# RWKV-7 with a hardswish feed-forward on one core: PSUM read in pairs of banks, and three steps moved in the head

## The chip, the core and the metric

One core of a Trainium2 chip runs the whole program. The metric is the device time in microseconds. Three runs of the kernel before took 807.92, 809.98 and 811.37 us; the median is 809.98. The engines are named as in the profile: PE multiplies matrices (PEld is its weight load), DVE, ACT and POOL work element by element, SP issues transfers, as ACT's queue also can.

## What is computed

```python
for t in range(S):                                   # S=768, per batch (4) and head (8), D=40
    y[:, :, t] = np.einsum('bhd,bhde->bhe', rt, state)
    Sa = np.einsum('bhde,bhe->bhd', state, at)
    state = state * wt[:, :, None, :] - np.einsum('bhd,bhe->bhde', Sa, bt) \
            + np.einsum('bhd,bhe->bhde', vt, kt)
x = y.transpose(0, 2, 1, 3).reshape(3072, 320)
h = x @ w_in                                          # 320 -> 2048
out = (h * np.clip(h + 3.0, 0.0, 6.0) / 6.0) @ w_out  # 2048 -> 320
```

The recurrence is in float32; the feed-forward weights arrive in 8-byte form and are turned to float32 on the chip.

## The kernel before, in words

Time is cut into blocks of 64 steps. A **unit** holds one such block of two batches and all 8 heads, 128 rows in all; there are 24 units, four to a group (NU = 4). Units 0 to 3 are the first group.

For each unit, `prepare` makes what doesn't depend on the state. Stage W transposes w on PE, ACT (for unit 0 DVE) copies it into `wm`, and a scan on DVE (L507) makes running products. Stage gam makes the reverse scan (L518) and fills the halves of `gam` and `rgam`, two by DVE (L526, L527) and two by POOL (L528, L529). A and B transpose a and b and multiply by `gam` and `rgam` on DVE (L544, L552), after a memset of some columns of `wm` (L541). F multiplies the two into a triangular matrix that ACT copies out of PSUM. K, factor, E and EV treat k and v: DVE copies E under a mask (`masked`, L483), POOL makes `KBt` (L621).

`invert` inverts the triangles of a group of four units. It begins with a DVE transpose `fb` (L679), makes some sixty dependent pairs of DVE instructions (L699, L705) and ends with two transposes `tb` and `tt` (L708, L713). Other DVE work is put between its instructions by `aside`. `third_blocks` (X for units 0 and 1, Y for 2 and 3) completes the inverse `tinv` with PE (L734, L757) and ACT (L742, L767). Before that, POOL sets all of `tinv` to zero (L1196), after the first two weight pieces, whose raw form lay there, have been converted.

`step` runs the part that depends on the state: RT and VT (transposes of r and v), C (a masked product of the two), R, U, UT, S, rS, sn (new state, L917), H (masked) and y; then `move` sends y as `xt` to the feed-forward by eight transfers on SP.

`feed_forward` yields pieces: `expand` (L1017, four pieces and a narrow rest, into two banks h), ACT and DVE make the activation (L1032, L1033), `contract` (L1058) sums into bank o. `pieces(n)` puts n of them into PE's program between the other products.

Weights come as 20 pieces of 512 KB through a few homes (`raw_homes`), loaded by SP (L294) when a home is free. Each piece is converted by four steps: DVE L316 with two ACT instructions, then DVE L336, L340 and L327. A `next(weights)` makes one step; STEPS lists the places in the first inversion at which one is made, and the numbers behind colons in PLAN the places in the first group's steps.

The order of the work is written out by hand: FIRST and BESIDE for the first group's preparation, with r of unit 0 fetched in slot 1 of BESIDE; then the inversion with the early steps (RT and VT of unit 0, RT and VT of unit 1, C of both, R of unit 0); then PLAN. r has one tile, so r of unit 1 is fetched by ACT inside `s_RT` of unit 0 (L793), when unit 0's r has been transposed. From unit 4 on, each unit takes four blocks; in each, `together` starts the products of a block and then finishes them, as far as five banks allow.

PSUM has eight banks. Two are h, one o, and five stand in one rotation, "any"; in the preparation of the first group h's two are in the rotation as well. `ps_any` takes the next single bank. `ps_pair` takes the next two, and a product's two halves go to different banks, so DVE or ACT reads it by two instructions, one for each bank.

Of the kernel before, what the change touches and what calls it, by code (L numbers as in the profile page):

```python
# [16 lines left out]
P = 128  # L17
BL = 64
# [12 lines left out]
def kernel(  # L31
# [67 lines left out]
    ring = deque([("any", 5)])  # L99

    def ps_any(shape):
        tag, bufs = ring[0]
        ring.rotate(-1)
        return bank(tag, shape, bufs)

# [3 lines left out]
    def ps_pair(*dims):  # L109

        n = 1
        for d in dims:
            n *= d
        if shared[0] is None or shared[1] + n > 512:
            shared[:] = [ps_any([P, 512]) for _ in range(2)], 0
        at = shared[1]
        shared[1] += n
        views, step = [], n
        for d in dims:
            step //= d  # L120
            views.append([step, d])
        return [_ap(t[:], at, views) for t in shared[0]]
# [20 lines left out]
    mask4 = _ap(mask[:], 0, [[0, 4], [1, BL]])  # L143
# [254 lines left out]
    def fetch(name, i, engine=None):  # L398

        if i is None or i >= NK:  # L400
            return
        x, crossed = {"W": (w, 0), "A": (a, 0), "B": (b, 0), "K": (k, 0), "R": (r, 1),
                      "V": (v, 1)}[name]
        if name == "V":
            t = values[i % AHEAD]
        else:
            t = placed.get((name, i))
            t = t if t is not None else (others if i < 2 * NU and i % 2 and name != "R" else inputs)[name]
        g, p = names[i]
        engines = engine or nc.sync  # L410
        for q in range(2):
            engine = engines[q] if isinstance(engines, tuple) else engines
            y = x[2 * p + q, :, g * BL:(g + 1) * BL, :]
            rows = slice(q * BL, (q + 1) * BL)
            if crossed:
                for s in range(2):
                    engine.dma_start(out=t[rows, 4 * s:4 * s + 4, 0:D],
                                     in_=y[s::2].rearrange("h t e -> t h e"))
            else:
                engine.dma_start(out=t[rows, :, 0:D], in_=y.rearrange("h t e -> t h e"))  # L420
        data[i][name + "N"] = t
# [29 lines left out]
    def in_halves(x):  # L451
        return [x[:, :, half(q)] for q in range(2)]

    def turn_in(x, halves):

        return turn_halves(x) if halves else [turn_pairs(x)[:]]

    def parts_of(x, halves):
        return in_halves(x) if halves else [x[:]]
# [19 lines left out]
    def masked(o):  # L479
        turn[0] += 1  # L480
        x = score[turn[0] % len(score)]
        for i in range(2):
            nc.vector.copy_predicated(out=x[:, 4 * i:4 * i + 4, :], mask=mask4, data=o[i])  # L483
        return x


    def prepare(i, F):
# [24 lines left out]
        def gam_stage():  # L512
# [13 lines left out]
            nc.vector.tensor_scalar(gv[:, :, 0:HB], _ap(o["wm"][:], HB + 1, [[row, NB], [-1, HB]]), 1.0, None, ALU.mult)  # L526
            nc.vector.tensor_scalar(rv[:, :, HB:BL], _ap(o["wm"][:], HB + 3, [[row, NB], [1, HB]]), 1.0, None, ALU.mult)  # L527
# [26 lines left out]
        def f_by_32():  # L554
# [15 lines left out]
            for s in range(2):  # L570
                x = n * H + 4 * s
                nc.scalar.activation(out=F[:, x:x + 4, :], in_=f[s], func=AF.Copy, scale=-1.0)

        def f_by_64():
# [10 lines left out]
            for s in range(2):  # L585
                x = n * H + 4 * s
                for z in range(0, P, BL):
                    nc.scalar.activation(out=F[z:z + L, x:x + 4, 0:L], in_=f[s][z:z + L, :, 0:L],
                                         func=AF.Copy, scale=-1.0)
                    y = f[s][z + L:z + BL].rearrange("p r (c t) -> p r c t", c=2)  # L590
                    nc.scalar.activation(
                        out=F[z + L:z + BL, x:x + 4, :].rearrange("p h (c t) -> p h c t", c=2),
                        in_=y[:, :, ::-1, :], func=AF.Copy, scale=-1.0)

        def factor_stage():
# [13 lines left out]
            if halves:  # L609
                for s in range(2):  # L610
                    nc.scalar.activation(out=rgt[:, s::2], in_=rg[s][:, :, 0:D], func=AF.Copy)  # L611
# [29 lines left out]
        def ev_stage():  # L641
# [10 lines left out]
            for q in range(2):  # L652
                for s in range(2):
                    nc.scalar.activation(out=EV[half(q ^ s), s], in_=ev[q][half(q ^ s)], func=AF.Copy)  # L654
# [123 lines left out]
    def step(i):  # L778
# [8 lines left out]
        def s_RT():  # L787
# [5 lines left out]
            fetch("R", i + 1, nc.scalar if i == 0 else None)  # L793
# [9 lines left out]
        def s_R():  # L803
# [13 lines left out]
            for s in range(2):  # L817
                nc.vector.tensor_tensor(out=R[:, s], in0=rp[s], in1=o["EV"][:, s], op=ALU.add)
# [25 lines left out]
        def s_U():  # L844
# [11 lines left out]
            for x in range(2):  # L856
                nc.scalar.activation(out=m["U"][:, 4 * x:4 * x + 4, 0:D], in_=up[x], func=AF.Copy,
                                     scale=-1.0)
# [6 lines left out]
        def s_UT():  # L865
# [13 lines left out]
            for x in range(2):  # L879
                nc.scalar.activation(out=m["UT"][:, 2 * x:2 * x + 2], in_=up[x], func=AF.Copy, scale=-1.0)  # L880

        def s_rS():
# [12 lines left out]
            for rs in range(2):  # L895
                nc.scalar.activation(out=ys[:, rs::2], in_=ysp[rs], func=AF.Copy)

        def s_sn():
# [15 lines left out]
            for q in range(2):  # L914
                for rows in [slice(0, P)] if i < NU else [half(s, D) for s in range(2)]:
                    x = st[rows, q, :, 0:D]
                    nc.vector.tensor_tensor(out=x, in0=sn[q][rows], in1=x, op=ALU.add)  # L917
# [6 lines left out]
        def s_y():  # L924
# [14 lines left out]
            if fresh:  # L939
                for q in range(2):  # L940
                    nc.vector.tensor_tensor(out=yg[:, :, half(q)], in0=y[q], in1=o["G"][:, :, half(q)],
                                            op=ALU.mult)
                return
            for q in range(2):
                nc.vector.tensor_tensor(out=m["ys"][:, :, q, :], in0=y[q],  # L945
                                        in1=m["ys"][:, :, q, :], op=ALU.add)
# [64 lines left out]
    def expand(xt, j0, gts):  # L1011

        hp = [bank("h", [P, NQ, P], 2) for _ in range(2)]
# [36 lines left out]
    def contract(i, r, gts):  # L1050
        split = i < SPLIT
        if r == 0 or split:
            op = bank("o", [P, DM], 1)
# [105 lines left out]
    ring.clear()  # L1159
    ring.extend([("any", 5)] * 5 + [("h", 2)] * 2)  # L1160
# [11 lines left out]
    for n, x in enumerate(BESIDE):  # L1172
# [3 lines left out]
        if n == 1:  # L1176
            fetch("R", 0)
        run(chains[int(x[0])], 1, MIXED if n >= 12 else 0)
    ring.clear()
    ring.append(("any", 5))  # L1180
# [6 lines left out]
    STEPS = (2, 4, 9, 12, 13, 16, 20, 24, 26, 31, 39, 52, 59, 61, 64)  # L1187
    n, cleared = 0, []
    while not third:
        aside(1)  # L1190
        if not third:
# [3 lines left out]
            if converted[0] >= 2 and not cleared:  # L1195
                cleared.append(nc.gpsimd.memset(tinv[:], 0.0))  # L1196
# [8 lines left out]
    def block(i, j):  # L1205

        if i % NU < 2:
            if j == 0:
# [6 lines left out]
    PLAN = """X:1 X:1 0U:3 0UT 1R  # L1215
              0sn:1 0H:2 Y:2
              1U 1UT:3 0y:2
              2RT:1 Y
              1sn:1 1H:1 2VT:1 0move 0move2
              1y:3 2R  # L1220
              2S:3 3RT:1
              1move 1move2 2U:1 2UT 2C:7
              3R:3 3VT:1
              2rS:3 2sn:3 2H:4 3S:2
              2y:3 3U:2 3UT:7 3C:5
              3rS:2 3sn:1 3H:2 2move
# [9 lines left out]
    for t, line in enumerate(plan):  # L1236
        for name, *amounts in line:
# [45 lines left out]
    def together(stages):  # L1283
# [3 lines left out]
        def finish():  # L1287
# [5 lines left out]
            shared[0] = None  # L1293

        for name in PRODUCTS:
            if name == FIRST_NARROW and narrow and spread[0] and stages:
                narrow[0]()
            for stage in stages.get(name, []):
                if name in TURNS:
                    need = 1  # L1300
# [109 lines left out]
```

## Time and profile before

| | |
|---|---|
| median of three runs | 809.98 us |
| the profiled execution | 807.46 us |
| its span, first to last instruction | 805.7 us |
| mean granted clock of PE | 0.947 of full speed |
| matmuls on PE | 15832 |
| DVE masked copies (L483), 128x256 | x142, mean 436 ns |
| DVE state (L917), 40x160 | x80, mean 321 ns |
| DVE activation (L1033), 128x512 | x96, mean 681 ns |
| ACT copies of UT (L880), 128x256 | x48, mean 395 ns |
| ACT copies of EV (L654), 64x160 | x88, mean 296 ns |
| DVE product kt (L634), 128x512 | x21, mean 687 ns |

A time in the profile is counted from the span's start. The profile's idle time before an instruction is given with what ended it; "issue" is time in which an engine waited for nothing that the profile shows.

### The profile page before, as it was taken

Reading aid. Unit: us, or ns where it says so; the run is one execution under the profiler, and the core shown is the slowest. Engines: PE = TensorE matmul, PEld = TensorE weight load, DVE = VectorE, ACT = ScalarE, POOL = GpSimd, SP = SyncE. Lnnn points to the kernel's source line nnn. Section 1 sums busy time; section 2 is a strip of 40 time slices with the busy share of each in tenths; the row PEclk is TensorE's granted clock in tenths of the full one; section 3 lists DMA queues with packets and bytes.
Section 4 is the critical chain, followed back from the end, with each engine's and each line's share of the span. In section 5 each row is a group of like instructions: output and inputs, shape, how many; then the busy total and the mean of one; then the engine's idle time right before and its main releaser. Section 6 shows DMA issues by size and latency. Waiting matters only on the chain.

```text
span 805.7 us, 35863 instructions
## 1 busy us (share of the span) xinstructions
PE 737.2 (91%) x15832; PEld 625.7 (78%) x15832; DVE 516.3 (64%) x1188; ACT 322.5 (40%) x852; POOL 177.2 (22%) x319
## 2 busy tenths in 40 slices
PE   4734868999999989999999999999999999999998
PEld 3724757878778868788878788888788888888886
DVE  8888977679556699555698446898355884332210
ACT  1344762321654524553434463435453324322111
POOL 6403012420222222223123123214123202000000
PEclk7755788999999999999999999999999999999999
DMA  9681663420223321233222233213222101110000
GB/s 121 120 192 55 152 167 59 79 44 9 51 51 66 62 53 31 49 63 59 38 45 40 46 58 61 46 35 56 45 47 49 19 20 29 30 25 13 15 19 16
DMA packets 174218, 45.05 MB, mean 56 GB/s; under 512 B 157424, under 2 KB 172784, under 8 KB 174064
## 3 DMA queue, kind: packets, MB, share of 16 engines
q1 hardware_dynamic: 168672, 41.87, 27.2%
q8 instruction: 125, 2.05, 1.0%
q10 hardware_dynamic: 5392, 0.90, 0.8%
q14 instruction: 29, 0.24, 0.1%
HBM read 34.08 MB, written 3.93 MB: 47 GB/s over the span
## 4 chain that ended last, share of the span: by engine, by line
PE 72%; DVE 10%; issue 5%; DMA 4%; ACT 2%; SPq 1%; POOL 1%; ACTq 0%; DVEq 0%; POOLq 0%
PE h L1017 25%; PE o L1058 23%; PE any L474 4%; PE any L436 3%; PE any L932 3%; PE any L446 2%; PE any L908 2%; DVE prod L699 2%; PE any L813 2%; DVE x L705 2%; PE any L852 1%; DMA R<-in_r_dram 1%; PE any L648 1%; PE any L873 1%; PE any L757 1%
## 5 line engine op out<-in xcount | busy, mean ns | idle before, releaser
L1017 PE MATMUL h<-xt,win 128*128 128x128 f32 (+1 forms) x2304 | 250.8, 282 | 5.8 <-DVE gt L1033 4.9
L1017 PEld LDWEIGHTS h<-xt,win 128*128 128x128 f32 (+1 forms) x2304 | 231.1, 192 | 23.4 <-issue 5.8
L1058 PE MATMUL o<-wout,gt 128*128 128x320 f32 x768 | 231.6, 445 | 0.0
L1058 PEld LDWEIGHTS o<-wout,gt 128*128 128x128 f32 x768 | 139.1, 191 | 50.9 <-issue 1.0
L1033 DVE SCALAR_TENSOR_TENSOR gt<-gt,h 128x512 f32<-128x512 f32 x96 | 62.0, 681 | 66.4 <-ACT gt L1032 66.2
L1032 ACT ACTIVATE gt<-h,three 128x512 f32<-128x512 f32 x96 | 62.1, 686 | 94.3 <-PE h L1017 94.0
L947 POOL TENSOR_TENSOR yg<-ys,gam 128x512 f32<-128x512 f32 x22 | 39.6, 1798 | 164.0 <-DVE ys L945 94.1
L917 DVE TENSOR_TENSOR state<-any,state 40x160 f32<-40x160 f32 (+1 forms) x88 | 27.9, 321 | 66.1 <-PE any L908 39.7
L699 DVE TENSOR_TENSOR prod<-x 128x30 f32<-128x30 f32 (+9 forms) x180 | 64.3, 357 | 8.6 <-POOL x L684 3.1
L705 DVE TENSOR_TENSOR x<-x,prod 128x30 f32<-128x30 f32 (+9 forms) x180 | 65.2, 362 | 5.4
L621 POOL TENSOR_TENSOR KBt<-K,rgt 128x320 f32<-128x320 f32 x22 | 19.1, 866 | 217.7 <-ACT rgt L611 214.1
L483 DVE COPY_PREDICATED score<-mask,any 128x256 f32<-128x256 int32 x142 | 53.0, 436 | 6.0 <-PE any L474 5.6
L945 DVE TENSOR_TENSOR ys<-any,ys 128x256 f32<-128x256 f32 x44 | 16.6, 419 | 34.8 <-PE any L648 18.3
L518 DVE TENSOR_TENSOR_SCAN wm<-wm,start 128x528 f32<-128x528 f32 x24 | 37.6, 1568 | 0.8
L792 ACT ACTIVATE RT<-any 128x256 f32<-128x256 f32 (+1 forms) x44 | 15.5, 401 | 54.8 <-PE any L446 48.7
L507 DVE TENSOR_TENSOR_SCAN prods<-wm,start 128x528 f32<-128x528 f32 x24 | 30.0, 1256 | 11.1 <-ACT wm L504 10.7
L654 ACT ACTIVATE EV<-any 64x160 f32<-64x160 f32 x88 | 23.9, 296 | 32.0 <-PE any L648 23.1
L932 PE MATMUL any<-score,KBt 64*64 64x64 f32 x1536 | 30.4, 229 | 3.1 <-DVE state L917 2.8
L932 PEld LDWEIGHTS any<-score,KBt 64*64 64x64 f32 x1536 | 26.7, 141 | 5.5 <-DVE state L917 3.0
L767 ACT ACTIVATE tinv<-any 32x256 f32<-32x256 f32 x48 | 18.0, 375 | 29.8 <-PE any L757 29.1
L528 POOL COPY gam<-prods 128x256 f32<-128x256 f32 x24 | 22.5, 938 | 29.9 <-DVE prods L507 26.0
L1076 ACT ACTIVATE ob<-o 128x320 f32<-128x320 f32 x22 | 9.6, 435 | 46.8 <-PE o L1058 29.2
(199 smaller groups left out, 1085.8 us busy)
## 6 DMA issues: line engine op xcount, KB each, us to landing
V<-in_v_dram SPq DMA_DIRECT2D x96, 40.0 KB
out_dram<-ob SPq DMA_DIRECT2D x47, 80.0 KB
R<-in_r_dram SPq DMA_DIRECT2D x92, 40.0 KB
B<-in_b_dram SPq DMA_DIRECT2D x42, 80.0 KB
K<-in_k_dram SPq DMA_DIRECT2D x42, 80.0 KB
W<-in_w_dram SPq DMA_DIRECT2D x37, 80.0 KB
A<-in_a_dram SPq DMA_DIRECT2D x37, 80.0 KB
xt<-yg SPq DMA_DIRECT2D x72, 40.0 KB
```

Source lines behind the costliest of these rows:

```text
L474: nc.tensor.matmul(out=o[i][half(q), n, :], lhsT=lhs[half(i, D), n ^ (2 * q * swap), half(q)], rhs=rhs[half(i, D), n, half(q)], start=True ...
L483: nc.vector.copy_predicated(out=x[:, 4 * i:4 * i + 4, :], mask=mask4, data=o[i])
L507: nc.vector.tensor_tensor_scan(out=prods[:].rearrange("p r m i -> p (r m i)"), data0=wm[:, 0:SCAN], data1=start[:], initial=0.0, op0=ALU.m ...
L518: nc.vector.tensor_tensor_scan(out=back, data0=back, data1=start[:], initial=0.0, op0=ALU.mult, op1=ALU.add)
L699: nc.vector.tensor_tensor(out=pv, in0=_ap(x[:], (i + 1) * L + i, [[L, n], [0, i]]), in1=_ap(x[:], i * L, [[0, n], [1, i]]), op=ALU.mult,)
L705: nc.vector.tensor_tensor(out=rest, in0=rest, in1=pv, op=ALU.add)
L932: nc.tensor.matmul(out=y[q][half(s), pr, :], lhsT=o[name][half(q), h * D:h * D + SLOT], rhs=m[name][half(q), 4 * rs + 2 * s + j, :], start ...
L947: nc.gpsimd.tensor_tensor(out=yg[:], in0=m["ys"][:].rearrange("p r q t -> p r (q t)"), in1=o["G"][:], op=ALU.mult)
L1017: nc.tensor.matmul(out=hp[c][:, i, :], lhsT=lhsT, rhs=rhs, start=(begun[c] == 0), stop=(begun[c] == 3 * NQ - 1))
L1032: nc.scalar.activation(out=gt[:], in_=hp[c][:], func=AF.Relu, bias=three[:], scale=1.0)
L1033: nc.vector.scalar_tensor_tensor(out=gt[:], in0=gt[:], scalar=6.0, in1=hp[c][:], op0=ALU.min, op1=ALU.mult)
L1058: nc.tensor.matmul(out=op[:], lhsT=gts[c][:, n, :], rhs=wout[:, c * HJ + r * NQ + n, :], start=((split or r == 0) and c == 0 and n == 0), ...
```

## The change

PSUM is handed out in pairs of neighbouring banks. A pair is one tile of two banks, and what lay in its two halves is read by one instruction with a wider access pattern: masked copies, RT, VT, at, bt, F, rgt, EV, R, U, UT, ys, the state and y. Up to the end of line 8 of PLAN there are three pairs (one of them "lent") and two single banks ("one" and o); from there the lent pair is h, and two pairs and "one" are left. In the preparation and in PLAN a single tile takes "one", o or a whole pair in turn; from unit 4 on, two single tiles share a pair.

r of unit 1 gets a tile of its own, the one that held k of unit 1. r of both units is fetched on SP in slot 4 of BESIDE. For units 0 to 3, ACT makes the two copies of `gam` and `rgam` that DVE made. The zero half of `tinv` is written by two ACT instructions instead of POOL's memset of the whole. STEPS and the numbers in PLAN differ.

```diff
-    ring = deque([("any", 5)])
+    ring, open_half = deque(), [None]
+    lent = tc.tile_pool(name="lent", bufs=1, space=PSUM)
+    pools = {"lent": lent.__enter__(), "pair": ps}
+    pairs = deque([("pair", 2), ("pair", 2), ("lent", 1)])
+
+    def pair():
+        pairs.rotate(-1)
+        tag, bufs = pairs[-1]
+        return pools[tag].tile([P, 2, 512], F32, name=tag, tag=tag, bufs=bufs)
+
+    def begun_ffn():
+        lent.__exit__(None, None, None)
+        pairs.clear()
+        pairs.append(("pair", 2))
+        pools["h"] = ctx.enter_context(tc.tile_pool(name="hidden", bufs=1, space=PSUM))
...
     def ps_any(shape):
         tag, bufs = ring[0]
         ring.rotate(-1)
-        return bank(tag, shape, bufs)
+        at = 0
+        if tag == "whole":
+            t = pair()
+            open_half[0] = None
+        elif tag != "pair":
+            t = bank(tag, [P, 512], bufs)
+        elif open_half[0] is None:
+            t = open_half[0] = pair()
+        else:
+            t, at = open_half[0], 512
+            open_half[0] = None
...
-            shared[:] = [ps_any([P, 512]) for _ in range(2)], 0
+            shared[:] = pair(), 0
+            open_half[0] = None
...
-        return [_ap(t[:], at, views) for t in shared[0]]
+        t = shared[0][:]
+        return [_ap(t, at, views), _ap(t, at + 512, views), _ap(t, at, [[512, 2]] + views)]
...
+            if (name, i) == ("R", 1):
+                t = others["K"]
...
-        for i in range(2):
-            nc.vector.copy_predicated(out=x[:, 4 * i:4 * i + 4, :], mask=mask4, data=o[i])
+        nc.vector.copy_predicated(out=x[:].rearrange("p (i h) t -> p i h t", i=2), mask=mask8, data=o[2])
...
-            nc.vector.tensor_scalar(gv[:, :, 0:HB], _ap(o["wm"][:], HB + 1, [[row, NB], [-1, HB]]), 1.0, None, ALU.mult)
-            nc.vector.tensor_scalar(rv[:, :, HB:BL], _ap(o["wm"][:], HB + 3, [[row, NB], [1, HB]]), 1.0, None, ALU.mult)
+            def copy(to, x):
+                if i < NU:
+                    nc.scalar.activation(out=to, in_=x, func=AF.Copy)
+                else:
+                    nc.vector.tensor_scalar(to, x, 1.0, None, ALU.mult)
+            copy(gv[:, :, 0:HB], _ap(o["wm"][:], HB + 1, [[row, NB], [-1, HB]]))
+            copy(rv[:, :, HB:BL], _ap(o["wm"][:], HB + 3, [[row, NB], [1, HB]]))
...
-            for s in range(2):
-                x = n * H + 4 * s
-                nc.scalar.activation(out=F[:, x:x + 4, :], in_=f[s], func=AF.Copy, scale=-1.0)
+            nc.scalar.activation(out=F[:, n * H:n * H + H, :].rearrange("p (s r) t -> p s r t", s=2), in_=f[2],
+                                 func=AF.Copy, scale=-1.0)
...
-            fetch("R", i + 1, nc.scalar if i == 0 else None)
+            if i:
+                fetch("R", i + 1)
...
-            for s in range(2):
-                nc.vector.tensor_tensor(out=R[:, s], in0=rp[s], in1=o["EV"][:, s], op=ALU.add)
+            nc.vector.tensor_tensor(out=R, in0=rp[2], in1=o["EV"][:], op=ALU.add)
...
-            for x in range(2):
-                nc.scalar.activation(out=m["UT"][:, 2 * x:2 * x + 2], in_=up[x], func=AF.Copy, scale=-1.0)
+            nc.scalar.activation(out=m["UT"][:].rearrange("p (x j) t -> p x j t", x=2), in_=up[2],
+                                 func=AF.Copy, scale=-1.0)
...
-    ring.extend([("any", 5)] * 5 + [("h", 2)] * 2)
+    ring.extend([("one", 1), ("whole", 2), ("o", 1), ("whole", 2)])
...
-        if n == 1:
+        if n == 4:
             fetch("R", 0)
+            fetch("R", 1)
...
-    STEPS = (2, 4, 9, 12, 13, 16, 20, 24, 26, 31, 39, 52, 59, 61, 64)
+    TURNS_IN = [("one", 1), ("pair", 2), ("pair", 2)]
+    STEPS = (1, 4, 9, 11, 12, 19, 21, 24, 28, 33, 44, 61, 64)
...
-                cleared.append(nc.gpsimd.memset(tinv[:], 0.0))
+                cleared.append(True)
+                for z in range(0, P, BL):
+                    nc.scalar.activation(out=tinv[z + L:z + BL, :, 0:L], func=AF.Copy, scale=0.0,
+                                         in_=_ap(three[z + L:z + BL], 0, [[0, NH], [0, L]]))
...
-    PLAN = """X:1 X:1 0U:3 0UT 1R
-              0sn:1 0H:2 Y:2
-              1U 1UT:3 0y:2
+    PLAN = """X X:1 0U:3 0UT:1 1R
+              0sn:1 0H:3 Y:1
+              1U 1UT:3 0y:1
...
+        if t == 8:
+            begun_ffn()
+            ring.clear()
+            ring.extend([("one", 1), ("whole", 2)])
...
-            shared[0] = None
+            shared[0] = open_half[0] = None
+            ring.clear()
+            ring.extend(TURNS_IN)
...
-                    need = 1
+                    need = 2 * (open_half[0] is None) if ring[0][0] == "pair" else 1
```

## The prediction

> **What bounds the kernel now.** I read the page's busy rows first, then busy time by stretch, then who waits for whom on PE, then the chain that ended last, and last the timelines of the engines on that chain.
>
> ```profile
> PE 737.2 (91%) x15832; PEld 625.7 (78%) x15832; DVE 516.3 (64%) x1188; ACT 322.5 (40%) x852; POOL 177.2 (22%) x319
> PE   4734868999999989999999999999999999999998
> DVE  8888977679556699555698446898355884332210
> ```
> ```profile
> 27.00:69.00 42.00, 17.39 (x412) 15.10 (x413) 37.66 (x91) 14.20 (x35) 11.13 (x22) 0.59 0.60 136
> 69.00:134.00 65.00, 48.30 (x1402) 43.38 (x1393) 55.74 (x116) 40.77 (x83) 14.79 (x26) 0.76 0.52 126
> 340.00:700.00 360.00, 355.41 (x8006) 303.73 (x8007) 234.16 (x547) 154.34 (x427) 83.98 (x137) 1.00 0.24 44
> ```
> Columns: length, then busy PE, PEld, DVE, ACT, POOL, granted clock, DMA share, GB/s. Two regimes. Up to about 134 us DVE is the busy engine (37.7 of 42 us, 55.7 of 65) and PE waits; from there PE is busy nearly always (355.4 of 360 us). The built program of after has PE's instructions in exactly the same order and number (8474 matmul-type entries; one transpose reads another tile). So a microsecond won before 134 us moves everything behind it; later, only a wait of PE counts:
>
> ```profile
> PE any L932 <- DVE state L917: 2.8, 1, 2.8
> PE h L1017 <- DVE gt L1033: 2.6, 3, 1.0
> PE any L580 <- ACT ys L896: 0.9, 1, 0.9
> PE any L813 <- DVE score L483: 0.7, 1, 0.7
> ```
> These are all of PE's waits for DVE or ACT after 133 us but 0.3; the first is the end of the head. About 4.5 us are left in 670 us. The chain through the head:
>
> ```profile
> 41.62 5.42 DMA R<-in_r_dram
> 50.94 3.11 DMA R<-in_r_dram
> 54.09 1.54 PE any L436 x6
> 66.31 1.91 DVE tb L708
> 115.26 6.38 DMA raw<-in_moe_w_out_dram
> 133.62 1.89 PE any L932 x61
> ```
> and DVE and ACT at its first half (start, length, engine; in brackets idle time and its releaser):
>
> ```profile
> 27.09 2.13 DVE L679 STREAM_TRANSPOSE fb<-F 128x1024 f32<-128x1024 f32 x1 [1.98 <-ACT F L572]
> 30.89 0.77 DVE L483 COPY_PREDICATED score<-mask,any 128x256 f32<-128x256 int32 x2
> 48.37 3.20 ACTq L417 DMA_DIRECT2D R<-in_r_dram  x4
> 56.75 0.77 DVE L483 COPY_PREDICATED score<-mask,any 128x256 f32<-128x256 int32 x2 [2.62 <-PE any L474]
> ```
> The first inversion runs on DVE from fb (27.09) to tb (66.31) with one real hole: 2.62 us before the mask of unit 0's C. Its matmuls stand on PE behind unit 1's r, which ACT could only issue at 48.37, once unit 0's r had left the same tile.
>
> **The change, part by part.** The sum is against the profiled execution, 807.46 us (span 805.7).
>
> *Pair reads.* DVE loses 194 instructions to merging and ACT 214. On DVE the mask pair at 30.89 lets the next instruction start at 31.55, so it costs 0.66 us; one 128x512 read of PSUM (kt, L634, mean 687 ns) lets the next start after 0.56 to 0.60 us. Saving 0.06 to 0.1 us. On ACT, the UT pair takes 0.67 us, one 128x512 copy (RT) 0.60. The Trainium skill (Perfetto Trace Analysis, Optimizing Scalar/DVE Operations) puts an instruction's own overhead on PSUM at about 125 ns on DVE and 51 on ACT: 24 us of DVE by the page, 12 to 19 by the rows; I take the rows. The same section speaks against the change: where DVE and ACT are not saturated but hold PE up, it advises breaking instructions up. By it, PE would lose what it could do on the first half: 0.69-0.44 = 0.25 us a hand-off. But the loops of L932, L908 and L889 touch both halves within some four to eight matmuls (64 matmuls of L932 take 1.09 us, so under 0.15 us), and the row at 56.75 shows the pair's end, 0.77, against 0.69 for one. I take -0.08 us a hand-off (ends: +0.15, -0.1). After 134 us DVE and ACT are half idle, so it is worth only a share of the 4.5 us: each gt wait is led by about six merged pairs (0.5 us), and F in 64-wide form goes from eight instructions to six (2.56 to 2.26 us). I take 1.5 us, bounds 0 and 4.5.
>
> *gam and rgam of units 0 to 3 on ACT.* DVE loses two instructions a unit, 0.41 us to the next start (11.51 to 11.92). ACT gains eight of 0.39 us (the wm copies, L500). A new wait: DVE's memset of wm (L541) waits for ACT to have read wm, and at and everything of DVE stand behind it. Unit 0: its scan would end 11.45, ACT is through at 12.3, DVE's next scan runs to 13.06: no wait. Unit 1: ACT ends 13.85, at of unit 0 ends 13.7: 0.15 us lost. Net 0.65 us for units 0 and 1. For 2 and 3 the ACT copies queue behind the F copies of units 0 and 1; net 0.5. Then F of units 2 and 3: four copies in 1.44 us become two, 1.15, on the chain into fb. Sum: fb starts 1.4 us earlier (bounds 0.7, 1.8).
>
> *r of unit 1 into K's place.* The four loads leave ACT (3.20 us at 48.37, with a weight conversion, VT and RT behind them) and stand on SP after unit 0's r, which keeps its place at 38.50. The tile is free long before (POOL's KBt of unit 1 ends 34.5). SP spaced its issues there by 0.64 to 1.3 us, so they go out from 43.6 to 47.2; B, K and nine weight loads slip by 3 us, to about 57, and SP was idle from 57.6 to 70.8; those weights are first read at 72.22. Unit 0's r still lands at 47.05, DMA-bound, whatever DVE does. Unit 1's was 3.1 us from its last issue to landing; so 49.5 to 50.3 now. RT, VT and C then follow as before (54.09 to 56.75 is 2.7 us): the mask at 52.9. DVE would arrive at 54.13-1.4-0.25 (four merged masks)-0.17 (a wait for ACT behind the r issues)=52.3. So the mask starts at 52.9, not 56.75: 3.9 us, of which the earlier fb is part (bounds: landing as late as 52 gives 1.4; DVE-bound gives 4.5).
>
> *T's zero half.* POOL's memset (1.81 us at 53.88) becomes two ACT copies of 32x1024 (L720: 1.06 us), 2.1 us. They wait for DVE's L327 at about 52; behind them on ACT stand RR (0.46) and a conversion that is not due before 60. ACT was idle 6.68 us there: nothing on the path; 2.1 us if that cover went.
>
> *Moved weight steps.* The conversions between instructions of the inversion are as many as before (12), two swapped with neighbours: nothing. One 512 KB load moves on SP from behind 12 transfers (109.14) to 100.6. It takes away DVE's 2.16 us wait at 113.79, but the next loads stay where SP reaches them, and the last weights still land at 121.7: that wait only moves down. The r and xt issues it overtakes slip 0.53 us. Perhaps 0.5 us, since the last load also waited 0.7 us for a piece that is now done sooner.
>
> From tb to 134 us SP issues without a hole from 86.5 to 115.8, begun by PE's L757, which hangs on tb. So tb's 3.96 us (3.9 and one more mask) pass through; merged U, UT, H, state give 0.3 more along it. Head: 4.0+0.3+0.5=4.8. With 1.5 later: **6.3 us**. 807.46-6.3=801.2 for such an execution; the median of the runs was 809.98, 2.5 above the profiled one, so 803.7 for the median.
>
> **Rivals.**
> - *The gain is swallowed by weights* (0.20). If unit 1's r shares the DMA engines with the weights behind it (0.82 of their time is busy from 40 to 60 us) and lands at 52, tb gains 1.4; if SP's train then starts no earlier or the last weights queue longer, 0 to 1.4 us arrives: about 809. For: that chain is DMA at 41.62, 50.94 and 115.26. Against: SP's train hangs on compute at both ends. That the pair reads do nothing of use later belongs here.
> - *Larger* (0.13): r at 48.5 leaves DVE alone as bound (4.5+0.8), and all 4.5 us of later waits go: 9.8 us, 800.
> - *Slower* (0.12): banks. Five free-standing banks in turn become one single and two pairs, the single first in each block. A block that held one transpose and one pair left the next block fresh banks; now its transpose waits for the same single bank's reader. Perfetto Trace Analysis (Matmuls) asks for rotation through banks so that evacuation overlaps; before, PE shows no such wait in steady state, and 1.75 to 3 pieces of feed-forward lie between blocks. An RT or W copy queued behind one 0.69 us gt on ACT would be its price. There are 80 blocks: from 0.08 us a block the 6.3 are gone; at 0.15, +12-6=+6 us, 816.
>
> **How the numbers follow.** The first case has 0.55, 801 to 806.5 for the median. A measurement tells about 0.5%, 4 us, from no change: faster means under 805.9. Of the first case 0.50 lies there, with the larger 0.13: 0.63. Within: 0.05+0.20+0.02=0.27. Slower: 0.10. Range 798 to 810.5, leaving out the slow case and the far end of the large one.
>
> **What would show it.** fb near 25.7; the transposes of unit 1's r near 50, with no ACT issue before them; the mask of C with under 1 us idle before; tb near 62.3; SP's busy train from about 82; last weights near 117; the end of the head (PE L932) near 129; later waits of PE for gt shorter. Wrong if tb moves and the last weights don't, if unit 1's r lands after 52, or if PE shows new waits at transposes in every block.

## The result, and the profile after

The changed kernel takes 802.65 us (median of 7 runs, 800.55 to 804.52); the kernel before took 809.98 us beside it (7 runs, 805.44 to 811.37). The ratio is 0.9923, interval 0.9896 to 0.995. The profiled execution took 802.65 us (span 800.6), 4.8 less than the one of before. The predicted 803.7 us is 1 us off; that it came so close is luck, since two errors of the working stood against each other, as the profile shows.

The busy rows of the profile's page, and its slices:

```profile
PE 734.8 (92%) x15832; PEld 624.2 (78%) x15832; DVE 501.2 (63%) x986; ACT 306.6 (38%) x648; POOL 177.0 (22%) x318
...
PE   5725878999999989999999999999999999999998
...
DVE  7898877679555699555698445897444983322210
```

DVE does 202 instructions fewer and 15.1 us less work. The three stretches (length, then busy PE, PEld, DVE, ACT, POOL, clock, DMA share, GB/s):

```profile
27.00:69.00 42.00, 14.84 (x428) 12.92 (x425) 39.34 (x88) 16.95 (x32) 11.92 (x24) 0.67 0.65 137
69.00:134.00 65.00, 49.54 (x1354) 44.62 (x1358) 53.19 (x99) 38.65 (x70) 11.87 (x23) 0.76 0.51 126
340.00:700.00 360.00, 358.15 (x8143) 305.99 (x8142) 225.62 (x440) 144.83 (x318) 83.86 (x136) 1.00 0.24 44
```

From 69 to 134 us DVE is busy 2.55 us less than before, and idle that much more: 11.81 us of the 65 instead of 9.26. In the last row PE is busy 2.7 us more of the same 360: there time is gained. The first half of the head on DVE, and on SP the load of unit 1's r:

```profile
26.34 2.12 DVE L718 STREAM_TRANSPOSE fb<-F 128x1024 f32<-128x1024 f32 x1 [2.08 <-ACT F L611]
...
40.60 0.43 DVE L349 TENSOR_SCALAR parts<-tinv 128x512 uint32<-128x512 uint32 x1 [1.18 <-DMA tinv<-in_moe_w_in_dram]
...
54.19 0.71 DVE L517 COPY_PREDICATED score<-mask,pair 128x512 f32<-128x512 int32 x1
```
```profile
44.41 3.67 SPq L452 DMA_DIRECT2D K<-in_r_dram  x4
```

The hole of 2.62 us before the mask of C is gone, but DVE reaches that mask at 54.19, as it did before (54.13): in its place it waited 1.18 us for a load of feed-forward weights at 40.60. The chain (start, length, what; not all of its pieces):

```profile
63.61 1.92 DVE tb L747
...
112.46 1.49 PE h L1051 x8
...
130.18 1.26 DVE wm L552
131.98 1.19 DVE gt L1067 x2
133.62 1.99 PE pair L969 x64
```

tb is 2.70 us earlier than before, and the end of the head (the last line) is where it was: 133.62 in both. What was won was lost again between 69 and 134 us. Now PE's waits after 133 us (waiting line, releaser: us in total, times, longest):

```profile
PE pair L969 <- DVE state L954: 3.1, 1, 3.1
PE pair L687 <- DVE score L517: 1.6, 1, 1.6
PE pair L687 <- issue: 1.5, 1, 1.5
PE pair L620 <- ACT ys L933: 1.2, 1, 1.2
PE pair L853 <- DVE score L517: 1.0, 1, 1.0
PE pair L687 <- PE pair L481: 1.0, 1, 1.0
PE pair L509 <- issue: 0.7, 2, 0.5
PE h L1051 <- DVE gt L1067: 0.6, 3, 0.2
```

gt's waits fell from 2.6 to 0.6 us, and new ones for merged readers (score) came. And two lines of the same view of before, which the prediction did not count since no releaser is named in them:

```profile
PE any L474 <- issue: 3.2, 3, 1.2
PE any L648 <- issue: 3.0, 3, 1.5
```

"issue" waits after 136 us sum to 7.1 us before and 3.0 after. Named waits other than those for gt grew meanwhile from 2.3 to 5.3 us, and some of that is only a new name: PE's stall of 1.49 us before its product at 173.79 (L648) is "issue" before, and after it is the 1.6 us for score in the list (L687, at 173.93).

### The profile page after: what moved, and what is told of

The parts are those of the page before. It is cut to its first block, busy times and chain, and to the rows that moved or that the text cites. A ratio compares the mean times of both kernels' runs of the same rounds, so it can differ in the third digit from the quotient of the medians.

```text
span 800.6 us, 35291 instructions
## 1 busy us (share of the span) xinstructions
PE 734.8 (92%) x15832; PEld 624.2 (78%) x15832; DVE 501.2 (63%) x986; ACT 306.6 (38%) x648; POOL 177.0 (22%) x318
## 3 DMA queue, kind: packets, MB, share of 16 engines
q8 instruction: 125, 2.05, 1.1%
## 4 chain that ended last, share of the span: by engine, by line
PE 79%; DVE 8%; issue 4%; DMA 3%; SPq 2%; ACT 2%; POOL 1%; DVEq 0%; POOLq 0%; ACTq 0%
PE h L1051 27%; PE o L1092 24%; PE pair L509 4%; PE pair L969 3%; PE one L471 3%; PE pair L946 2%; PE pair L481 2%; PE pair L853 2%; PE pair L891 2%; DVE wm L552 1%; PE pair L687 1%; PE pair L927 1%; SPq L327 1%; PE pair L796 1%; PE pair L911 1%
## 5 line engine op out<-in xcount | busy, mean ns | idle before, releaser
L738 DVE TENSOR_TENSOR prod<-x 128x30 f32<-128x30 f32 (+9 forms) x180 | 67.1, 373 | 8.7 <-POOL x L723 3.3
L744 DVE TENSOR_TENSOR x<-x,prod 128x30 f32<-128x30 f32 (+9 forms) x180 | 62.2, 345 | 5.4
L954 DVE TENSOR_TENSOR state<-pair,state 40x320 f32<-40x320 f32 (+1 forms) x44 | 21.5, 488 | 64.9 <-PE pair L946 38.6
L517 DVE COPY_PREDICATED score<-mask,pair 128x512 f32<-128x512 int32 x71 | 49.8, 722 | 0.9 <-PE pair L509 0.5
L980 DVE TENSOR_TENSOR ys<-pair,ys 128x512 f32<-128x512 f32 x22 | 15.2, 690 | 43.4 <-PE pair L687 22.0
L969 PE MATMUL pair<-score,KBt 64*64 64x64 f32 x1472 | 29.3, 231 | 4.2 <-DVE state L954 3.1
L831 ACT ACTIVATE RT<-pair 128x512 f32<-128x512 f32 x21 | 12.5, 597 | 52.9 <-PE pair L481 52.9
L692 ACT ACTIVATE EV<-pair 64x320 f32<-64x320 f32 x44 | 19.0, 432 | 34.3 <-PE pair L687 23.7
L969 PEld LDWEIGHTS pair<-score,KBt 64*64 64x64 f32 x1472 | 25.8, 143 | 7.0 <-DVE state L954 3.6
L806 ACT ACTIVATE tinv<-pair 32x256 f32<-32x256 f32 x48 | 18.0, 374 | 31.5 <-PE pair L796 30.9
```

What stands on the lines that cost most here:

```text
L517: nc.vector.copy_predicated(out=x[:].rearrange("p (i h) t -> p i h t", i=2), mask=mask8, data=o[2])
L738: nc.vector.tensor_tensor(out=pv, in0=_ap(x[:], (i + 1) * L + i, [[L, n], [0, i]]), in1=_ap(x[:], i * L, [[0, n], [1, i]]), op=ALU.mult,)
L744: nc.vector.tensor_tensor(out=rest, in0=rest, in1=pv, op=ALU.add)
L969: nc.tensor.matmul(out=y[q][half(s), pr, :], lhsT=o[name][half(q), h * D:h * D + SLOT], rhs=m[name][half(q), 4 * rs + 2 * s + j, :], start ...
```

## The experiments

Two theories went in. A: the head passes its gain on, as predicted. B: the head's gain is lost before 134 us, and the time is won later. Each kernel is compared with the kernel before on the same chip. The marks of every profiled execution, in us (weights: DVE's start on the first feed-forward weights with its wait for their load; C: idle of DVE before the mask of unit 0's C; gt: DVE's first gt with its wait for ACT; last: DVE's start on the last piece of weights; head: its end; rest: PE from its matmul 2160, near 139 us, to its last). The 4.0 to 6.5 us between head and rest are in neither column; they differ with the clock that PE was granted there (last section).

| kernel | weights | C | tb | gt | last | head | rest |
|---|---|---|---|---|---|---|---|
| before | 40.21 (0) | 2.62 | 66.31 | 110.34 (0.29) | 121.74 | 133.62 | 662.4 |
| before, again | 41.09 (1.47) | 2.86 | 67.58 | 112.17 (0.28) | 123.67 | 135.55 | 660.1 |
| after | 40.60 (1.18) | 0 | 63.61 | 111.72 (2.60) | 121.63 | 133.62 | 657.3 |
| after, again | 40.72 (1.48) | 0 | 63.74 | 110.89 (2.60) | 121.19 | 133.19 | 657.9 |
| pairs only | 41.26 (0.82) | 1.54 | 65.92 | 113.00 (2.60) | 123.49 | 135.50 | 657.8 |
| moves only | 40.73 (1.85) | 0 | 63.85 | 109.28 (0.28) | 119.91 | 131.81 | 660.6 |
| r only | 41.19 (1.15) | 0 | 64.87 | 110.35 (0.28) | 121.81 | 133.70 | 661.3 |
| gam only | 40.23 (0.39) | 1.88 | 65.34 | 109.34 (0.28) | 121.96 | 134.56 | 660.3 |
| old deals | 40.27 (1.06) | 0 | 63.29 | 108.34 (0.33) | 119.34 | 132.09 | 657.4 |
| U first | 39.85 (0.60) | 0 | 62.88 | 108.00 (0.33) | 119.23 | 131.24 | 656.4 |
| U and ys first | 41.48 (2.40) | 0 | 64.51 | 107.82 (1.05) | 121.40 | 133.39 | 658.2 |
| late DVE split | 42.32 (2.95) | 0 | 65.35 | 112.63 (2.60) | 123.13 | 135.12 | 660.4 |
| late ACT split | 42.15 (2.69) | 0 | 65.19 | 111.68 (2.60) | 122.17 | 134.17 | 658.3 |
| late both split | 40.68 (1.36) | 0 | 63.70 | 111.66 (2.60) | 122.15 | 134.14 | 662.8 |

Each row is one execution, and some lie well off the median of their kernel's runs: before 2.5 us below it, old deals 3.0 and U first 2.2 below, late DVE split 2.0 above.

**The two kernels again**, unchanged.

> The kernel before, unchanged, for a second profile. Both theories: span 803 to 809 us; tb near 66.3; the matmuls of y that end the head (PE L932) near 133.6 us. If the waits of PE named issue (at 172, 245, 339, 458, 575 us in the first profile) are places in the program, they stand there again within 0.3 us each; if they are chance, they are elsewhere or gone.

> The changed kernel, unchanged. Theory A (the head passes its gain on, and the first profile of it was an unlucky one in the head): the end of the head near 129 to 131 us. Theory B (the head's gain is always lost again before 134 us and the gain is made later): again 133.2 to 134.0 us with tb near 63.6, and a span near 800. Time in both 799 to 804.5, ratio to before 0.990 to 0.995.

Measured: before 807.3 us in one run (the 22 runs of before on that chip have a median of 808.03); after 802.99, ratio 0.9937 (0.9918 to 0.9957). The gain stands. Of the five "issue" stalls asked about, the one near 458 us is gone; the other four stand before the same products again, 0.2 to 3.5 us later. The first profile of before had a piece of luck that the prediction took for the rule: it alone of the 14 executions has no wait of DVE for the first weights' load. Of before again:

```profile
41.09 0.43 DVE L316 TENSOR_SCALAR parts<-tinv 128x512 uint32<-128x512 uint32 x1 [1.47 <-DMA tinv<-in_moe_w_in_dram]
```

**The change in halves.** Pairs only: the changed kernel, with gam on DVE, r of unit 1 on ACT's queue and T's memset on POOL as before. Moves only: the kernel before (its banks, reads and deals of weight work) with

```
+            if (name, i) == ("R", 1):
+                t = others["K"]
...
-            fetch("R", i + 1, nc.scalar if i == 0 else None)
+            if i:
+                fetch("R", i + 1)
...
-        if n == 1:
+        if n == 4:
             fetch("R", 0)
+            fetch("R", 1)
...
-                cleared.append(nc.gpsimd.memset(tinv[:], 0.0))
+                cleared.append(True)
+                for z in range(0, P, BL):
+                    nc.scalar.activation(out=tinv[z + L:z + BL, :, 0:L], func=AF.Copy, scale=0.0,
```

and the copies of gam on ACT.

> Pairs of banks and one read for each pair, with the STEPS and PLAN of the changed kernel; r of unit 1 again by ACT into r's tile, gam and rgam by DVE, T zeroed by POOL. Theory A: tb near 66 and only the later share of the gain, 1.5 us: ratio about 0.998. Theory B: the whole gain, or nearly: ratio 0.991 to 0.994, with the end of the head at 133 to 135 us and the gain after 180 us.

> The other half: single banks, two reads and the STEPS and PLAN of before, but r of unit 1 in k's tile from SP, gam and rgam of units 0 to 3 by ACT, T's zero half by ACT. Theory A: 3.5 to 4.5 us, ratio about 0.995, tb near 63. Theory B: tb near 63 too, but the end of the head within 0.7 us of 133.6 and no gain at the end: ratio 0.998 to 1.001.

Measured: pairs only 804.93 us, 0.9958 (0.9938 to 0.9978); moves only 804.92, 0.9963 (0.9947 to 0.9979). Both ratios lie between what the two theories expected: each half is worth some 3 us, by different ways. The moves win in the head: tb 63.85, its end 131.81 against 133.62 and 135.55, and nothing after it (660.6, inside the 660.1 to 662.4 of before). The pairs win nothing in the head (135.50) and some 3 us after it (657.8, against a mean of 660.9 in the five executions with the old banks). Together the head ends at 133.62 and 133.19, later than with the moves alone. So theory B holds for the sum, and the loss belongs to the half with the pairs, which carries the new deals.

**The moves one by one.** r only is the first three edits above on the kernel before; gam only is the copies of gam on it.

> The kernel before with r of unit 1 in k's tile, loaded by SyncE, and nothing else of the change. If the early r is what the moves are worth (all of them together gave 0.9963): tb at 64 to 65 instead of 67, the end of the head 1.5 to 2.5 us earlier, ratio 0.9965 to 0.998. If the copies of gam on ScalarE or T's zero half carry it: tb within 0.5 us of 67 and ratio 0.999 to 1.001.

> The kernel before with gam and rgam of units 0 to 3 copied by ScalarE, and nothing else of the change. All moves together gave 0.9963 and r alone 0.9985. If the copies of gam are the other half: fb 0.6 to 0.8 us earlier, ratio 0.9975 to 0.999. If T's zero half on ScalarE (which leaves POOL free) is the other half: ratio 0.9995 to 1.001.

Measured: r only 807.7 us, 0.9985 (0.997 to 1.0): the mask of C no longer waits, tb 64.87, but the head's end, at 133.70, only beats the second execution of before, and the ratio lies between its two expectations. gam only 806.91, 0.9989 (0.9976 to 1.0002): fb at 26.62, 0.3 to 0.5 us earlier, not 0.6 to 0.8. Each interval touches no change. 1.2 and 0.9 us leave 0.9 of the moves' 3.0 for T's zero half or for the moves together; that edit was not run alone, and 0.9 us is less than these intervals can tell.

**The old deals.** The changed kernel with STEPS and PLAN, the two hand-written deals of weight work, as they were before:

```
-    STEPS = (1, 4, 9, 11, 12, 19, 21, 24, 28, 33, 44, 61, 64)
+    STEPS = (2, 4, 9, 12, 13, 16, 20, 24, 26, 31, 39, 52, 59, 61, 64)
...
-    PLAN = """X X:1 0U:3 0UT:1 1R
+    PLAN = """X:1 X:1 0U:3 0UT 1R
```

> The changed kernel with the two hand-written deals of the weight work (STEPS and PLAN) of the kernel before. Theory P: the changed kernel loses some 2.5 us of its head at 104 to 112 us because its deals let a weight conversion on ScalarE and S stand before the gelu of the feed-forward block (gt), for which VectorE and then PE wait 2.60 and 4.07 us; with the old deals gt stands first again. By P the end of the head (PE's wait before the first 64 matmuls of the output product) comes near 131 instead of 133.6, and the ratio to the kernel before is 0.989 to 0.991. Rival Q: the old deals have their own 2.2 us wait for the last weights' DMA in the same place, and the head is bound by them: its end stays at 133 to 134 and the ratio at 0.9925 to 0.9945.

(What is called gelu there is the hardswish of the activation.) First the loss itself, on ACT in the profile of after:

```profile
109.15 0.72 ACT L350 ACTIVATE parts<-parts,low 128x512 f32<-128x512 int32 x1 [1.01 <-DVE parts L349]
109.91 0.72 ACT L352 ACTIVATE parts<-parts,low 128x512 int32<-128x512 f32 x1
110.53 0.58 ACT L880 ACTIVATE S<-pair 128x512 f32<-128x512 f32 x1
111.01 1.26 ACT L1066 ACTIVATE gt<-h,three 128x512 f32<-128x512 f32 x2
```

on DVE:

```profile
108.70 0.41 DVE L349 TENSOR_SCALAR parts<-raw 128x512 uint32<-128x512 uint32 x1
111.72 1.28 DVE L1067 SCALAR_TENSOR_TENSOR gt<-gt,h 128x512 f32<-128x512 f32 x2 [2.60 <-ACT gt L1066]
```

and on PE:

```profile
112.46 1.49 PE L1051 MATMUL h<-xt,win 128*128 128x128 f32 x8 [4.07 <-DVE gt L1067]
```

The new PLAN puts a conversion (DVE 108.70, ACT 109.15 and 109.91) ahead of gt. ACT comes to S and gt only behind it, DVE stands idle 2.60 us at gt, and PE 4.07 (2.30 in before, 2.05 with the old deals). In before, gt came first and DVE waited for the load behind it:

```profile
110.34 1.28 DVE L1033 SCALAR_TENSOR_TENSOR gt<-gt,h 128x512 f32<-128x512 f32 x2 [0.29 <-ACT gt L1032]
113.79 0.43 DVE L316 TENSOR_SCALAR parts<-raw 128x512 uint32<-128x512 uint32 x1 [2.16 <-DMA raw<-in_moe_w_out_dram]
```

All six executions with the new deals have this 2.60; the five of kernels with the banks and deals of before have 0.28 or 0.29. With the old deals, on DVE:

```profile
108.34 1.28 DVE L1067 SCALAR_TENSOR_TENSOR gt<-gt,h 128x512 f32<-128x512 f32 x2 [0.33 <-ACT gt L1066]
...
119.34 0.43 DVE L349 TENSOR_SCALAR parts<-raw 128x512 uint32<-128x512 uint32 x1
...
131.56 0.48 DVE L954 TENSOR_TENSOR state<-pair,state 128x320 f32<-128x320 f32 x1
```

Measured: 802.47 us, 0.9911 (0.9897 to 0.9926); span 797.8, and the end of the head at 132.09. The mechanism of theory P is there, at the edge of its ratio; its place (near 131) is missed by 1 us. Both intervals of the changed kernel overlap this one: the times alone do not prove the old deals better, while the head's end in the trace is 1.1 to 1.5 us earlier, in one execution that was 3.0 us faster than the median of its runs.

**What ends the head.** U first: the old deals, and in them

```
-              2y:3 3U:2 3UT:7 3C:5
+              2y:3 3U 3UT:4 3C:10
```

U and ys first: 3S:2, 2y:3 3U:2 3UT:7 3C:5 become 3S:1, 2y:1 3U 3UT:6 3C:11.

> The changed kernel with the old deals of the weight work, and in them ScalarE's copies of U and UT of unit 3 each one weight conversion earlier (3U:2 3UT:7 3C:5 becomes 3U 3UT:4 3C:10). In the trace with the old deals PE waits 2.71 us at 117.48 for that U, which stands behind a conversion that itself waits for a load. If a wait that is taken away there reaches the end of the head: the 2.7 us wait is gone, the end of the head comes 1.5 to 2.7 us earlier than with the old deals alone (near 129.5 to 130.5), ratio 0.987 to 0.990. Rival: the next wait (feed-forward weights converted later, or the state update) takes its place; the head ends as with the old deals and the ratio stays at 0.990 to 0.993.

> As the run before it, and besides VectorE's gt and ys stand before the conversion that waits for its load, and U before two conversions (3S:2, 2y:3 3U:2 3UT:7 3C:5 become 3S:1, 2y:1 3U 3UT:6 3C:11). The wait for ys of 0.64 us goes too: 0.3 to 0.6 us more than the run before it if the last weights, converted up to 1.2 us later, are still in time; if they are late, PE waits for wout at the first product of the feed-forward output and the ratio is 0.002 to 0.004 worse than in the run before it.

Measured: U first 801.03 us, 0.9917 (0.9896 to 0.9939); U and ys first 803.14, 0.9935 (0.9916 to 0.9954). In U first PE's wait of 2.71 us for U is gone, and PE is there 3 us earlier, to wait longer at the end:

```profile
122.32 0.69 PE L927 MATMUL pair<-RT,S 40*64 40x64 f32 x32 [1.20 <-ACT wm L538]
...
131.24 1.99 PE L969 MATMUL pair<-score,KBt 64*64 64x64 f32 x64 [5.32 <-DVE state L954]
```

The wait had been 2.36 us with the old deals. So the rival of that run is right in the main: of 2.7 us, 0.85 arrived at the head's end, 0.41 of it already there in tb. U and ys first lost 1.63 us against U first by tb, where DVE waited 2.40 us for the first weights; from tb to the head's end it took 68.9 us against 68.4, so its two further edits gain nothing. What ends the head is DVE: from the last piece of weights it works without a hole (conversion, the scans of the next group's decays, gt, state), and the state starts 11.45 to 11.52 us after "last" in 12 of the 14 executions. In the other two it is 12.22; there a scan waits for ACT, 0.40 us in gam only and 0.67 with the old deals. A change that leaves the last weights' turn where it is leaves the head's end where it is: 121.74 before, 121.63 after.

**Where the later gain is.** The changed kernel, with reads of units 4 and later split in two again: by DVE only, by ACT only, by both. The banks stay as changed. For the mask:

```
+        if i >= NU:
+            for j in range(2):
+                nc.vector.copy_predicated(out=x[:, 4 * j:4 * j + 4, :], mask=_ap(mask[:], 0, [[0, 4], [1, BL]]),
+                                          data=o[j])
+            return x
```

and likewise for at, bt, R, state and ys on DVE, and for RT, VT, F, rgt, EV, U, UT and ys on ACT.

> The changed kernel with VectorE's reads of PSUM pairs split in two again for units 4 and later only (masks, at, bt, R, state, outputs: 174 more instructions on VectorE, none before some 135 us); the banks stay paired. Theory M: the late gain (3.5 to 4 us after some 300 us) comes from fewer instructions on VectorE before gt; then the ratio goes back to 0.9955 to 0.998, and PE's waits for gt after 132 us come back from 0.6 to about 2 us. Rival B: the late gain comes from the layout of the banks, or from ScalarE's merged copies; then the ratio stays at 0.9925 to 0.9945 and the waits at 0.6.

> The changed kernel with ScalarE's reads of PSUM pairs split in two again for units 4 and later only (transposed r and v, F, rgt, EV, U, UT, outputs: 203 more instructions on ScalarE, none before some 135 us); the banks stay paired. Theory M2: the late gain comes from fewer instructions on ScalarE before its half of gt; then the ratio goes back to 0.9955 to 0.998 and PE's waits for gt or for ScalarE after 132 us grow from 0.6 to 2 us or more. Rival B: bank layout; the ratio stays at 0.9925 to 0.9945.

> The changed kernel with VectorE's and ScalarE's reads of PSUM pairs both split in two again for units 4 and later; what is left of the change after 135 us is the layout of the banks (pairs, and one fixed turn of banks per block). From the end of the head to the end of the last matmul PE took 660.1 to 662.4 us in five kernels with the old banks and 656.4 to 658.2 us in six with pairs and merged reads. If the layout carries the late gain: PE's stalls without a visible releaser before the score products near 245, 339, 457 and 575 us (0.6 to 1.4 us each) stay away, the waits for gt come back at most in part, and the late part is 658 to 659.5 us. If the merged reads carry it: these stalls come back, and the waits for gt with 2.6 us, and the late part is 660 to 662 us.

Measured: DVE split 804.75 us, 0.9944 (0.9927 to 0.9962); ACT split 803.63, 0.993 (0.9917 to 0.9943); both 805.77, 0.9975 (0.9961 to 0.9989). The first two ratios lie where theory B expected them, and taken alone they would have said that the layout of the banks carries the late gain. The third run refutes that: without any merged read after the head, 3 to 4 us of the gain are gone (0.9975 against 0.9923 and 0.9937, the intervals apart), and PE's rest is 662.8 us, no less than the 660.1 to 662.4 with the old banks, though a stretch of lower clock near 251 us is in it (last section). Either engine's merged reads alone get part of it back (660.4 with ACT's, 658.3 with DVE's), both together 657.3 to 657.9; these are one execution each. PE's waits after 137 us when both are split:

```profile
PE pair L702 <- issue: 4.8, 3, 1.8
PE h L1093 <- DVE gt L1109: 2.5, 3, 1.0
PE pair L814 <- DVE score L523: 1.5, 4, 0.6
```

The waits for gt are back with 2.5 us; with DVE alone split they stay at 0.8, with ACT alone at 1.6. So either engine's shorter queue is enough to bring part of gt in time, and the first of the three waits (0.7 us near 283 us) hangs on ACT alone.

All executions have PE's matmuls in the same order and number, so they can be laid side by side, 48 matmuls at a time. The three stretches with a wait for gt, near 283, 402 and 520 us, are on average 0.76, 0.60 and 0.61 us shorter in the six executions with pairs and merged reads than in the five with the old banks; with both split they are as long as with the old banks, within 0.06 us. That is 2.0 of the 3.4 us between the two means, and the merged reads make it.

One expected sign did not come: PE's stalls near 245, 339, 457 and 575 us (the first before h, the others before score products) stay away in all kernels with pairs, split or not. The stretches that held them take 2.7, 0.7, 0.8 and 0.8 us in all nine, and up to 4.0, 2.3, 2.0 and 2.1 us with the old banks; on average the four are 4.3 us shorter. But waits elsewhere take 3.3 us back: behind the one near 339 us a stall of 0.2 to 0.8 us has come in all nine, and a new one of 0.2 to 0.8 near 544 in seven. One of the old stalls in the kernel before, on PE (start, length; idle in brackets):

```profile
338.85 0.65 PE L474 MATMUL any<-RT,UT 40*64 40x64 f32 x28
340.54 0.27 PE L474 MATMUL any<-RT,UT 40*64 40x64 f32 x2 [1.04 <-issue]
```

and what DVE did then:

```profile
339.00 1.35 DVE L917 TENSOR_TENSOR state<-any,state 40x160 f32<-40x160 f32 x4 [7.66 <-PE any L908]
```

PE goes on 0.19 us after DVE's fourth state read ends (340.35). That fits a wait for the bank that this read empties, which the profile does not name; it was not tested by itself. After, the state takes two reads, 0.99 us, and this stall is not there; nor is it where the state takes four reads again (late DVE split, late both split), so the number of reads alone does not make it. The layout took these stalls away and put others in their place (the L702 line above); only with merged reads is the balance a gain.

## Why the prediction was right, and where it was not

The total was 6.3 us; by the two ratios it is 5.1 to 6.2 us, by the medians 7.3. But the sum was to be head 4.8 and later 1.5. Measured: later 3.4 us (mean rest of 660.9 in five executions with the old banks, 657.5 in six with pairs and merged reads; 3.0 us without the stretch near 174 us, where the clock differed), and in the head 0 us between the two profiled executions, 0.5 if all executions with these heads are averaged (134.6 before, 134.1 in after, its repeat and the three late splits). The head was put 4.3 to 4.8 us too high and the later part 1.5 to 1.9 too low. What was measured adds up to 3.0 to 3.9 us, less than the 5.1 to 6.2 of the ratios: both profiled executions of before were faster than the median of the runs beside them (2.5 and 0.7 us), and where the rest lies is open.

- *fb.* Predicted 1.4 us earlier; it was 0.75. That term is worth nothing where DVE then waits for the first weights' load, as in 13 of 14 executions. In all eight executions with every move and the pairs, tb comes 23.01 to 23.04 us after DVE's start on those weights, whatever fb was (25.98 to 26.38). The bound of the first half is that DMA's landing, which my step "DVE would arrive at 52.3" left out since the one profile of before had no such wait.
- *r of unit 1.* Unit 0's r did not land as before: PE could start on it at 48.33, not at 47.19. The transpose of unit 1's r was predicted near 50 and came at 50.07; the hole before the mask of C is gone. The mask came at 54.19 instead of 52.9: DVE was last after all, by the load just told. tb won 2.7 us against one execution of before and 4.0 against the other, not the sure 3.96.
- *T's zero half.* Two ACT copies took 2.12 us at 54.27, and RR followed at 56.40. No wait for them is seen; not shown by a run alone.
- *Moved weight steps.* This is the step that failed. I wrote that the earlier load takes DVE's 2.16 us wait away and that this wait "only moves down", with last weights near 117. The wait did go, and not down: DVE has no DMA wait there in after. Its place was taken by 2.60 us for gt, since with the load the conversion moved too: one DVE and two ACT instructions (1.4 us) ahead of S and gt. I counted the moved DMA and not the ACT work that hangs on it. The last weights had their turn at 121.63. That tb moves and the last weights don't was named above as a sign of being wrong, and it came.
- *tb passes through to 134.* Wrong, in part for the same reason: from tb to the head's end it is 67.3 and 68.0 us before, 70.0 and 69.5 after, 68.8 with the old deals. Over all executions it is 69.0 to 70.4 with the new deals (six, mean 69.7) and 67.3 to 69.2 with the old ones (eight, mean 68.4). So the new deals account for some 1.3 of the 2.7 us lost between the first two profiles; for the rest, that execution of before was the quickest of all 14 here.
- *Merged reads.* In pairs only, DVE's time is 13.2 us less (516.3 to 503.1) for the 194 merged instructions, inside the predicted 12 to 19; the 15.1 us of the whole change have in them the copies of gam that ACT took over. Their worth after the head was mis-sized: 3.0 to 3.4 us for 1.5. gt's waits gave 2.0 us of that. The rest is a balance that I had not counted: stalls without a releaser that went, and new waits that came.
- *The slower rival* had something in it. The Trainium skill (Perfetto Trace Analysis, Matmuls) wants rotation through banks so that evacuation overlaps with the next products; with pairs and split reads PE's rest was 662.8 us in its one profile, so the layout alone brought nothing there against the free banks. The price that the rival named, waits at transposes in every block, is not seen: after 136 us no wait of PE stands before transposes (L471, L481) in after. The merged reads are worth 3 to 4 us on top of the layout, by the ratios. The same page's remark that breaking up instructions may let work finish sooner where DVE and ACT are not saturated but hold other engines up (Optimizing Scalar/DVE Operations), weighed in the prediction, is not borne out here: in the rest DVE is busy 63% and ACT 40% of the time (225.62 and 144.83 of 360 us), both hold PE up, and breaking their reads up cost 3 to 4 us by the ratios.

Open are the cause of the "issue" stalls and of the waits that came with the pairs, T's zero half by itself, and whether the old deals are better by more than the trace shows of one execution each.

## What to carry to other kernels

Before a stretch is credited with a saving on its busy engine, find the next transfer that this engine needs, and look at more than one execution: a wait of zero in one profile was 0.4 to 2.95 us in thirteen others. When a load is moved forward, follow the conversion that hangs on it through every engine's queue, and see what it now stands in front of. Pairs of banks and single instructions that empty them belong together: the layout without the merged reads gave nothing after the head.

## What was not expected of the hardware

Near 174 us the same 48 matmuls took 4.52 to 4.66 us in eight of the 14 executions and 3.25 to 3.29 in the other six; after has it, its repeat does not. It is no wait: the four products for the output among these matmuls take about twice as long each (0.53 us to the next start, not 0.27), and the clock that PE was granted is lower. In after and in its repeat, from 174 to 177 us (the 0.60 and the 1.00 are the clock):

```profile
174.53 2.49 PE L1092 MATMUL o<-wout,gt 128*128 128x320 f32 x4
174.00:177.00 3.00, 3.00 (x40) 1.70 (x40) 2.61 (x7) 0.86 (x2) 0.85 (x2) 0.60 0.57 95
```
```profile
175.09 1.35 PE L1092 MATMUL o<-wout,gt 128*128 128x320 f32 x4
174.00:177.00 3.00, 2.38 (x65) 1.67 (x68) 2.83 (x7) 0.86 (x2) 1.42 (x2) 1.00 0.44 74
```

PE had waited just before in both, 1.61 and 1.59 us; what decides between them is not shown. Four of the five executions with the old banks have it and three of the six with pairs and merged reads, which makes 0.5 of the 3.4 us between the means. With both reads split it stands near 251 us instead (clock 0.57 from 251 to 255 us), where 96 matmuls took 4.28 us against 3.10 and 3.58 in the two other splits. Right behind the head the same is seen: before had a clock of 0.50 from 134 to 137 us, the old deals 1.00 from 132 to 136. So one pair of profiles leaves a gain of a few microseconds uncertain by one or two; the granted clock by stretch, and the same stretch in 14 executions side by side, settle it.
